# Three row outputs of set 8 in the buffers of the products E, and the rounded angle of the last two quarters in the tile u

## The chip, the core and the metric

The kernel runs on one core of one Trainium2 chip. The metric is the device time of one launch in microseconds (us). Five engines work side by side, each in the order of its own instructions: TensorE (PE in the profile, with its weight loads as PEld), VectorE (DVE), ScalarE (ACT), GpSimd (POOL) and SyncE (SP), which issues nearly all DMAs.

## What is computed

The reference is an adaLN block: a state space convolution (S4D) over 2048 tokens of 448 channels, and behind it a token-mixing MLP.

```python
x = A_u                                              # (1, 2048, 448)
sa, ca, ga, sb, cb, gb = modulation of c by w_mod
h = _layernorm(x) * (1 + ca) + sa
x = x + ga * _A_ref(h, ...)
h = _layernorm(x) * (1 + cb) + sb
x = x + gb * _B_ref(h, ...)                          # W2 gelu(W1 h), over the tokens
...
def _A_ref(u, log_A_real, A_imag, C_real, C_imag, log_dt, D_skip):
    dt = exp(log_dt); A = -exp(log_A_real) + 1j * A_imag; C = (C_real + 1j * C_imag) * dt
    P = exp((A * dt)[:, :, None] * pos)              # 448 channels x 256 modes x 2048 positions
    K = 2.0 * einsum("dn,dnl->dl", C, P).real
    y = irfft(rfft(u, 4096) * rfft(K, 4096))[:2048]
    return y + u * D_skip
```

## The kernel before

The kernel makes the convolution kernel K in 56 **steps** (two per group of 16 channels). A step s takes phases and magnitudes of 128 modes and makes two products: E (VectorE, lines 718 to 722) and G (GpSimd, lines 716 and 717). TensorE multiplies them into K two steps later (`st_kgen`, line 743). Eight steps are a **set** (sets 0, 8, 16, 24, ...). Ahead of each set stands a **window** (`window(s)`): ScalarE makes the eight magnitudes (`mag`, exponentials), and then changes its table for the sines of the steps. In a window no product is made, so E's buffers are idle there. E has three buffers of 128 x 2 x 16 x 64 floats, used in turn; step s takes the next one.

Other work is threaded between. In the windows of sets 8 and 16 and the steps behind them TensorE makes the **row outputs** of the spectrum of the input (`u_rows`, line 571): row outputs come in pairs, VectorE scales each of a pair out of PSUM into a tile `yt` (line 574), and a DMA writes the pair of 128 x 896 floats to DRAM (`yu_d`, line 576). There are 16 pairs, and `yt` has three buffers. Six of the pairs are made in the window of set 8. In the same window TensorE makes a first part of K's spectrum (`y`, line 781), which ScalarE copies (`yk`, line 787). PSUM has three banks for row outputs, modulation and `y` together (tag `ms`). From set 16 on the **column outputs** follow (`pu` at line 606, scaled into `uo` by VectorE at line 610).

The parameters come in four **quarters** q of 128 channels (the last has 64). `chain(q)` turns raw parameters into the tables that the phases need, a few VectorE instructions at a time. Its tiles have one buffer each per quarter. `split` takes a value apart into a rounded part and a rest (`hl`, lines 400 and 402, two buffers) and sends both to DRAM (`pars`, line 406); inside a window, and for q = 1, GpSimd does it, else VectorE. `phase` writes the tile `p64` and splits it; `angles` then rounds the angle `xa` into a tile and subtracts it (lines 438 and 440). For q = 1 `phase` stands ahead of the logarithms, for which u is needed afterwards; for q = 2 and 3 it stands at the end, when u is no longer needed but for the rounding inside `phase`.

The order on TensorE, ScalarE, VectorE and GpSimd is the order of the code (`manual_schedule`). SyncE's is so until step 8, and set by the framework's planner after that. Buffers of a pool are taken in turn; an instruction that writes a buffer waits for the last reader of what was in it.

Behind the steps come the products of the spectra (`pc_...`), a stretch with many transfers, then layernorm and the MLP, whose matmuls (lines 1377 to 1379 and 1540 to 1542) fill the last 270 us.

Of the kernel before, what the change touches and what calls it, by code (L numbers as in the profile page):

```python
# [11 lines left out]
F32 = mybir.dt.float32  # L12
# [3 lines left out]
ALU = mybir.AluOpType  # L16
# [5 lines left out]
L, D, N, F = 2048, 448, 256, 1792  # L22
P = 128
# [3 lines left out]
NI, NJ = 32, 64  # L27
GD = 16
# [5 lines left out]
MAGIC = 1.5 * 2.0**23  # L34
# [198 lines left out]
def tile_adaln_s4d_mixer(ctx, tc, i, out):  # L233
# [19 lines left out]
    with ExitStack() as es:  # L253
        V, S, G, T = nc.vector, nc.scalar, nc.gpsimd, nc.tensor
        tt, ts, stt = V.tensor_tensor, V.tensor_scalar, V.scalar_tensor_tensor
# [20 lines left out]
        xp = spec.enter_context(tc.tile_pool(name="xp", bufs=1))  # L276
# [110 lines left out]
        def chain(q):  # L387


            n = min(P, D - P * q)  # L390
            f = N * n // P
            cr, ci, a, aim = (raws[q][nm][:, 0:f] for nm in ("A_C_real", "A_C_imag", "A_log_A_real", "A_A_imag"))
            xa, ya, s, t, u, ph, p64 = (
                qp.tile([P, N], F32, tag=nm, name=nm)[:, 0:f] for nm in ("xa", "ya", "s", "t", "u", "ph", "p64")
            )

            def split(src, places):
                hl = qp.tile([P, 2, N], F32R, tag="hl", name="hl", bufs=2)[:, :, 0:f]
                eng = G if aside or q == 1 else V
                eng.tensor_copy(hl[:, 0], src)  # L400
                yield
                eng.tensor_tensor(hl[:, 1], src, hl[:, 0].bitcast(F32), ALU.subtract)
                for k, v in places:
                    for m in range(P // n):
                        to = pars[q][v, k, 0:n, :, m * f : (m + 1) * f]
                        nc.sync.dma_start(to, hl[n * m : n * m + n].bitcast(F32))
                yield


            def phase():  # L410
                ts(ph, aim, dt4[:, q : q + 1], None, ALU.mult)
                yield
                ts(u, ph, MAGIC, MAGIC, ALU.add, ALU.subtract)
                yield
                tt(ph, ph, u, ALU.subtract)
                yield
                yield from split(ph, [(0, 0)])

                ts(u, ph, MAGIC7, MAGIC7, ALU.add, ALU.subtract)
                yield  # L420
                tt(p64, ph, u, ALU.subtract)
                yield
                yield from split(p64, [(1, 0)])

            def angles():
                ts(xa, xa, 4 * i2p, -0.5, ALU.mult, ALU.add)
                yield
                ts(cr, cr, 0.0, 0.5, ALU.is_ge, ALU.subtract)
                yield
                tt(xa, xa, cr, ALU.mult)  # L430
                yield
                ts(ci, ci, 0.0, 0.5, ALU.is_ge, ALU.subtract)
                yield
                stt(xa, xa, 0.5, ci, ALU.add, ALU.mult)
                yield
                stt(xa, ph, 63.0, xa, ALU.mult, ALU.add)
                yield
                ts(p64, xa, MAGIC, MAGIC, ALU.add, ALU.subtract)
                yield
                tt(xa, xa, p64, ALU.subtract)  # L440
                yield
                yield from split(xa, [(2, 0)])

            for to, src in (xa, cr), (ya, ci):
                if q > 1:
                    S.activation(to, src, AF.Abs, scale=0.5)
                else:
                    ts(to, src, -0.5, None, ALU.mult)
                    yield
                    stt(to, src, 0.5, to, ALU.mult, ALU.max)  # L450
                    yield
            tt(s, xa, ya, ALU.add)
            yield
            tt(ya, ya, xa, ALU.subtract)
            yield
            ts(s, s, 2.0**-120, None, ALU.max)
            yield
            V.reciprocal(xa, s)
            yield
            tt(ya, ya, xa, ALU.mult)  # L460
            yield

            ts(t, s, 2.0**-40, 2.0**80, ALU.is_lt, ALU.mult)
            yield
            stt(s, t, 1.0, s, ALU.max, ALU.mult)
            yield
            if q == 1:
                while not late_steps:
                    yield "logs"
                yield from phase()  # L470
            tmp[q] = a, s, u, xa, ya
            while q in tmp:
                yield "logs"
            if q == 1:
                yield from angles()
            ya = u
            yield from split(a, [(0, 1), (1, 1)])
            stt(s, t, -80 * math.log(2.0) / 2.0**80, s, ALU.mult, ALU.add)
            yield
            stt(s, ya, 0.5, s, ALU.mult, ALU.add)  # L480
            yield
            ts(s, s, ldt2[:, q : q + 1], None, ALU.add)
            yield
            yield from split(s, [(2, 1)])
            yield "exponents"

            if q > 1:
                yield from phase()

            if q > 1:  # L490
                yield from angles()
# [59 lines left out]
            tt(rs, rs, nm, ALU.mult)  # L551
            ts(xt[:, :, D : D + 1], mv[:, :, 0:1], -1.0, None, ALU.mult)

        yts, wurs = {}, {}

        def u_table(R):
            wurs[R] = xp.tile([P, 2, P], F32, tag="wur", name="wur", bufs=3)
            scales = rs[:, 2 * R : 2 * R + 2, None].to_broadcast([P, 2, P])
            G.tensor_tensor(wurs[R], wu[:, None, :].to_broadcast([P, 2, P]), scales, ALU.mult)

        def u_rows(n):

            R, g = divmod(n, 4)
            gp, gl = divmod(g, 2)
            if gl == 0:
                yts[R, gp] = xp.tile([P, 2, D], F32, tag="yt", name="yt", bufs=3)
            if g == 0 and R < 6:
                u_table(R + 2)
            pm = pms.tile([P, D + 1], F32, tag="ms", name="pu")
            p = slice(64 * gl, 64 * gl + 64)  # L570
            T.matmul(pm, wurs[R][p, gp], xt[p, 2 * R + gp, 0 : D + 1], start=True, stop=True)

            def out():
                stt(yts[R, gp][:, gl], pm[:, 0:D], pm[:, D : D + 1], mod[1], ALU.add, ALU.mult)
                if gl:
                    nc.sync.dma_start(
                        yu_d[:, :, :, R, 2 * gp : 2 * gp + 2].rearrange("o k c g d -> (o k c) (g d)"),
                        yts.pop((R, gp)).rearrange("p g d -> p (g d)"),
                    )

            dve.append(out)
# [489 lines left out]
        def window(s):  # L1071
# [12 lines left out]
            for e in range(BATCH):  # L1084
# [33 lines left out]
                if s in (8, 16):  # L1118
                    some(u_rows, rows, ((0, 2, 2, 2, 2, 0, 2, 2) if s == 8 else (2, 2, 2, 2, 2, 0, 1, 1))[e])
                elif s == 24 and e in (0, 2, 4, 6, 7):  # L1120
                    some(u_cols, cols, 1)
# [21 lines left out]
        for s in range(NHALF):  # L1143
# [13 lines left out]
            if s % BATCH == 0:  # L1157
                (late_window if s > 32 else window)(s)
                if s == 0:
                    gp_ = right("gp", 3)  # L1160
# [56 lines left out]
            if 8 <= s < 16 and free:  # L1217
                some(u_rows, rows, 2 if s % 2 else 3)
# [47 lines left out]
        n = pieces[0]  # L1266
# [47 lines left out]
        for k in range(NP + 1):  # L1314

            n = NP + k
# [42 lines left out]
    with ExitStack() as es:  # L1359
# [169 lines left out]
        for t in range(16):  # L1529
# [4 lines left out]
            for kh in range(2):  # L1534
                n = 32 + 2 * t + kh
# [38 lines left out]
```

## Time and profile before

| | |
|---|---|
| median of 3 runs | 670.04 us (669.04 to 670.37) |
| profiled execution, time | 668.55 us |
| its span, first to last instruction | 666.7 us |
| TensorE busy | 615.8 us (92%) |
| VectorE busy | 442.9 us (66%) |
| ScalarE busy | 440.4 us (66%) |
| GpSimd busy | 269.7 us (40%), all of it in the first 55% of the span |
| mean granted TensorE clock | 0.978 |

Durations of single instructions are from the one profiled execution. A row of the timeline reads: start, length, engine, line, operation, output and inputs, size, count, and in brackets how long the engine was idle before and what ended that. In the chain of waits a row is start, length and what the time went to. A row of a stretch gives the busy time of each engine in it.

### The profile page before, as it was taken

To read this page: it belongs to the slowest core of one execution; us is meant where nothing else is said; L and a number is where in the kernel's file an instruction comes from. 1 tells how busy PE (TensorE), PEld (TensorE's weight loads), DVE (VectorE), ACT (ScalarE), POOL (GpSimd) and SP (SyncE) were. 2 spreads that over 40 slices of the span, in tenths; PEclk is the share of its full clock that TensorE was granted. 3 is DMA by queue.
4 is the path that set the end of the run, shared out by engine and by line. 5 is a ranking of instruction groups with operands and counts; after the bars stand their busy time and mean duration, and the time that the engine had idled before them with its cause. 6 is when DMAs were issued, how large, how long until landed. Compare 5 with 4: busy or idle time off the path is not lost.

```text
span 666.7 us, 19151 instructions
## 1 busy us (share of the span) xinstructions
PE 615.8 (92%) x7637; PEld 445.0 (67%) x7637; DVE 442.9 (66%) x850; ACT 440.4 (66%) x828; POOL 269.7 (40%) x349
## 2 busy tenths in 40 slices
PE   1868899999899999999989899999999999999997
PEld 0545455445346565656645577788999999999997
DVE  8989789689696686869655678787522553333331
ACT  6978698899689999999678678886222532222220
POOL 7885588488589878797463000000000000000000
PEclk9998899999899899999999899999999999999999
DMA  6696747598775458567787999946664265555530
GB/s 157 191 215 174 253 157 247 197 257 260 221 236 175 107 128 215 168 185 222 210 281 238 262 243 249 220 125 200 169 189 137 71 188 161 165 162 167 163 116 28
DMA packets 99601, 125.14 MB, mean 188 GB/s; under 512 B 13780, under 2 KB 81144, under 8 KB 99512
## 3 DMA queue, kind: packets, MB, share of 16 engines
q1 hardware_dynamic: 98568, 121.30, 63.9%
q0 software_dynamic: 944, 2.62, 1.6%
q8 instruction: 60, 0.98, 0.6%
q14 instruction: 29, 0.24, 0.1%
HBM read 88.53 MB, written 34.87 MB: 185 GB/s over the span
## 4 chain that ended last, share of the span: by engine, by line
PE 60%; DMA 13%; ACT 9%; POOL 6%; DVE 5%; issue 4%; SPq 2%; ACTq 0%; DVEq 0%; POOLq 0%
PE o L1541 7%; PE o L1540 7%; PE o L1542 7%; PE acc L1377 6%; PE acc L1378 6%; PE acc L1379 6%; PE xe L646 5%; PE kg L743 5%; DMA v_d<-vt 4%; DMA w<-in_B_w_dram 3%; PE xg L646 3%; DMA lph<-pars 2%; PE pu L606 2%; PE vv L874 2%; POOL G L716 2%
## 5 line engine op out<-in xcount | busy, mean ns | idle before, releaser
L218 ACT CAST whi<-w 128x896 fp32r<-128x896 f32 x64 | 59.7, 939 | 138.2 <-PE o L1541 81.3
L227 DVE TENSOR_TENSOR wlo<-w,whi 128x896 fp32r<-128x896 f32 x64 | 68.1, 1086 | 41.2 <-ACT whi L218 38.1
L716 POOL TENSOR_TENSOR G<-mag,gs 128x512 f32<-128x512 f32 x56 | 71.9, 1284 | 42.2 <-ACT gs L712 42.2
L1377 PE MATMUL acc<-h3h,whi 128*128 128x448 f32 x224 | 83.0, 370 | 2.4 <-ACT h3h L1444 0.9
L1378 PE MATMUL acc<-h3l,whi 128*128 128x448 f32 x224 | 81.6, 364 | 0.6 <-DVE h3l L1451 0.4
L1541 PE MATMUL o<-ul,whi 128*128 128x448 f32 x224 | 81.3, 363 | 0.0
L1540 PE MATMUL o<-uh,whi 128*128 128x448 f32 x224 | 81.2, 362 | 0.0
L1379 PE MATMUL acc<-h3h,wlo 128*128 128x448 f32 x224 | 80.7, 360 | 0.0
L1542 PE MATMUL o<-uh,wlo 128*128 128x448 f32 x224 | 80.6, 360 | 0.0
L743 PEld LDWEIGHTS kg<-E,G 128*32 128x32 f32 x3584 | 54.7, 112 | 30.2 <-issue 19.0
L717 POOL TENSOR_TENSOR G<-mag,gs 128x512 f32<-128x512 f32 x56 | 71.9, 1284 | 0.0
L646 PE MATMUL xg<-tab,lph 64*128 64x512 f32 x112 | 63.4, 566 | 8.2 <-DVE E L722 5.3
L743 PE MATMUL kg<-E,G 128*32 128x64 f32 x3584 | 63.9, 224 | 4.8 <-issue 3.4
L646 PE MATMUL xe<-tab,lph 64*128 64x512 f32 x112 | 63.5, 567 | 0.3 <-issue 0.2
L1545 DVE TENSOR_TENSOR y<-o,x 128x448 f32<-128x448 f32 x16 | 10.0, 627 | 78.9 <-PE o L1542 78.9
L696 POOL TENSOR_TENSOR m<-mag,w 128x512 f32<-128x512 f32 x53 | 55.8, 1053 | 4.1
L1377 PEld LDWEIGHTS acc<-h3h,whi 128*128 128x128 f32 x224 | 42.0, 188 | 16.1 <-ACT h L1449 2.8
L708 ACT ACTIVATE ab<-xe 128x512 f32<-128x512 f32 x56 | 33.8, 604 | 19.5 <-PE xg L646 10.2
L1378 PEld LDWEIGHTS acc<-h3l,whi 128*128 128x128 f32 x224 | 42.1, 188 | 3.6 <-DVE h3l L1451 1.0
L1540 PEld LDWEIGHTS o<-uh,whi 128*128 128x128 f32 x224 | 42.0, 188 | 3.4
L1542 PEld LDWEIGHTS o<-uh,wlo 128*128 128x128 f32 x224 | 41.9, 187 | 3.0
L1379 PEld LDWEIGHTS acc<-h3h,wlo 128*128 128x128 f32 x224 | 41.9, 187 | 2.9
(249 smaller groups left out, 1406.6 us busy)
## 6 DMA issues: line engine op xcount, KB each, us to landing
w<-in_B_w_dram SPq DMA_DIRECT2D x64, 224.0 KB
w<-in_B_w_dram SPq DMA_DIRECT2D x32, 448.0 KB
yu_d<-yt SPq DMA_DIRECT2D x16, 448.0 KB
yi<-yu_d SPq DMA_DIRECT2D x32, 224.0 KB
us_d<-uo SPq DMA_DIRECT2D x16, 448.0 KB
u<-us_d SPq DMA_DIRECT2D x64, 112.0 KB
v_d<-vt SPq DMA_DIRECT2D x32, 224.0 KB
vt<-v_d SPq DMA_DIRECT2D x14, 448.0 KB
```

Source lines behind the costliest of these rows:

```text
L218: self.nc.scalar.copy(hi, w)
L227: eng.tensor_tensor(lo, w, hi.bitcast(F32), ALU.subtract)
L646: T.matmul(out[k], lhs[r], rhs[r], start=start, stop=stop)
L716: G.tensor_tensor(Gt[:, 1], mg_, v32(sg), ALU.mult)
L717: G.tensor_tensor(Gt[:, 0], mg_, v32(cg_), ALU.mult)
L743: T.matmul(kg[32 * q : 32 * q + 32, m], Gt[:, c, d], E[:, c, d], start=h == 0 and c == 0 and m == 0, stop=h == 1 and c == 1, skip_group_ch ...
L1377: nc.tensor.matmul(acc[f], hi[:, fs], h3h[:, r], start=r == 0, stop=False)
L1378: nc.tensor.matmul(acc[f], hi[:, fs], h3l[:, r], start=False, stop=False)
L1379: nc.tensor.matmul(acc[f], lo[:, fs], h3h[:, r], start=False, stop=r == 15)
L1540: nc.tensor.matmul(o, hi[:, ks], uh[kh][:, k], start=kh == 0 and k == 0, stop=False)
L1541: nc.tensor.matmul(o, hi[:, ks], ul[kh][:, k], start=False, stop=False)
L1542: nc.tensor.matmul(o, lo[:, ks], uh[kh][:, k], start=False, stop=kh == 1 and k == 6)
```

## The change

Two edits. In `u_rows` the third, fourth and fifth pair of row outputs (counted from 0: pairs 2 to 4) are not written into `yt` but into two buffers that are taken from the pool of E: pairs 2 and 3 share one, pair 4 has the other. The buffers of `yt` are so taken by pairs 0, 1, 5, 6, ... in turn. In `angles` the rounded angle of the quarters 2 and 3 goes into u instead of p64.

```diff
@@ angles(), in chain(q)
-                ts(p64, xa, MAGIC, MAGIC, ALU.add, ALU.subtract)
+                whole = u if q > 1 else p64
+                ts(whole, xa, MAGIC, MAGIC, ALU.add, ALU.subtract)
                 yield
-                tt(xa, xa, p64, ALU.subtract)
+                tt(xa, xa, whole, ALU.subtract)
@@
-        yts, wurs = {}, {}
+        yts, wurs, lent = {}, {}, []
@@ u_rows(n)
             if gl == 0:
-                yts[R, gp] = xp.tile([P, 2, D], F32, tag="yt", name="yt", bufs=3)
+                pair = n // 2
+                if pair in (2, 4):
+                    E = gp_.tile([P, 2, GD, NJ], F32, tag="E", name="yE")
+                    rooms = E.rearrange("p a g j -> p (a g j)")[:, 0 : 4 * D].rearrange("p (h g d) -> p h g d", h=2, g=2)
+                    lent.extend(rooms[:, h] for h in range(2))
+                yts[R, gp] = lent[pair - 2] if 2 <= pair < 5 else xp.tile([P, 2, D], F32, tag="yt", name="yt", bufs=3)
```

No instruction changes its place on any engine, SyncE's queue included; what changes is what some of them wait for. In the rows below the names in brackets are the semaphores waited for: DMAHW0 to 7 stand for DMAs, the others for engines. Line numbers of the change are 1 to 6 higher.

VectorE in the window of set 8, before: the pairs of row outputs 1 to 4, with the start of the chain of q = 2 between the last two.

```order
L574 SCALAR_TENSOR_TENSOR yt<-pu,mod_105 128x448 [waits PE_49] x4
L574 SCALAR_TENSOR_TENSOR yt<-pu,mod_105 128x448 [waits DMAHW7_49,PE_49]
L574 SCALAR_TENSOR_TENSOR yt<-pu,mod_105 128x448 [waits PE_49]
L452 TENSOR_TENSOR s<-xa,ya 128x256 [waits DVE_49,Activation_49,Pool_49]
L454 TENSOR_TENSOR ya<-ya,xa 128x256 [waits DVE_49]
L456 TENSOR_SCALAR s<-s 128x256
L458 RECIPROCAL xa<-s 128x256 [waits DVE_49]
L460 TENSOR_TENSOR ya<-ya,xa 128x256 [waits DVE_49]
L463 TENSOR_SCALAR t<-s 128x256
L574 SCALAR_TENSOR_TENSOR yt<-pu,mod_105 128x448 [waits DMAHW0_49,PE_49]
L574 SCALAR_TENSOR_TENSOR yt<-pu,mod_105 128x448 [waits PE_49]
```

The same place now:

```order
L580 SCALAR_TENSOR_TENSOR yt<-pu,mod_105 128x448 [waits PE_49] x2
L580 SCALAR_TENSOR_TENSOR yE<-pu,mod_105 128x448 [waits PE_49] x4
L453 TENSOR_TENSOR s<-xa,ya 128x256 [waits DVE_49,Activation_49,Pool_49]
L455 TENSOR_TENSOR ya<-ya,xa 128x256 [waits DVE_49]
L457 TENSOR_SCALAR s<-s 128x256
L459 RECIPROCAL xa<-s 128x256 [waits DVE_49]
L461 TENSOR_TENSOR ya<-ya,xa 128x256 [waits DVE_49]
L464 TENSOR_SCALAR t<-s 128x256
L580 SCALAR_TENSOR_TENSOR yE<-pu,mod_105 128x448 [waits PE_49] x2
```

The waits for the DMAs of earlier pairs are gone from pairs 3 and 4 (counted from 0).

VectorE in the steps 9 and 10, now: the first products E that come into the borrowed buffers.

```order
L724 TENSOR_TENSOR E<-m_1112,xe 128x16x32 [waits DMAHW3_49,DMAHW2_49,Activation_49]
L725 SCALAR_TENSOR_TENSOR E<-mag,xe 128x16x32
L727 TENSOR_TENSOR E<-mag,xg 128x16x32 [waits Activation_49]
L728 TENSOR_TENSOR E<-m_1112,xg 128x16x32
L724 TENSOR_TENSOR E<-m_1353,xe 128x16x32 [waits DMAHW6_49,Activation_49,Pool_49]
```

Their waits for DMAHW3, DMAHW2 and DMAHW6 are new.

VectorE at the end of the window of set 24, before: the last instructions of `angles` for q = 3, and two pairs of column outputs.

```order
L436 SCALAR_TENSOR_TENSOR xa<-ph,xa 128x128 [waits DVE_49]
L438 TENSOR_SCALAR p_2172<-xa 128x128 [waits DVE_49,Pool_49]
L440 TENSOR_TENSOR xa<-xa,p_2172 128x128 [waits DVE_49]
L610 SCALAR_TENSOR_TENSOR uo<-mod_104,svt,pu 128x2x224 [waits DMAHW1_49,PE_49]
L610 SCALAR_TENSOR_TENSOR uo<-mod_104,svt,pu 128x2x224 [waits PE_49]
```

The same place now:

```order
L439 TENSOR_SCALAR u<-xa 128x128 [waits DVE_49]
L441 TENSOR_TENSOR xa<-xa,u 128x128 [waits DVE_49]
L616 SCALAR_TENSOR_TENSOR uo<-mod_104,svt,pu 128x2x224 [waits DMAHW1_49,PE_49]
L616 SCALAR_TENSOR_TENSOR uo<-mod_104,svt,pu 128x2x224 [waits PE_49]
L616 SCALAR_TENSOR_TENSOR uo<-mod_104,svt,pu 128x2x224 [waits DMAHW2_49,PE_49]
```

The wait for GpSimd (Pool) has gone from the rounding. The first products E of steps 24 and 25, and the first instruction of the next quarter's chain, carry a wait for GpSimd that the old row used to cover.

## The prediction

> **What bounds the kernel now.** I read the page first, then the chain of work that ended last, then the timeline around the two places that the change touches, and last the table of stretches.
>
> ```profile
> span 666.7 us, 19151 instructions
> PE 60%; DMA 13%; ACT 9%; POOL 6%; DVE 5%; issue 4%; SPq 2%; ACTq 0%; DVEq 0%; POOLq 0%
> ```
>
> The chain is mostly TensorE, but it changes hands. Around the first place, the window of set 8, it runs over these pieces:
>
> ```profile
> 70.94 5.08 DMA yu_d<-yt
> ...
> 76.12 0.70 DVE yt L574
> ...
> 82.92 1.28 ACT L711
> ```
>
> So the chain comes through a DMA that writes a row output to DRAM, because its buffer is wanted again. Two stretches behind the two places show what takes the time once the windows are over (columns: PE, PEld, DVE, ACT, POOL busy, each with its count, then the granted clock, DMA share, GB/s):
>
> ```profile
> 85.40:109.90 24.50, 23.79 (x458) 13.72 (x450) 22.46 (x38) 21.99 (x44) 24.03 (x27) 1.00 0.59 194
> 186.60:210.80 24.20, 23.27 (x570) 13.32 (x572) 23.35 (x40) 22.38 (x44) 23.77 (x25) 1.00 0.56 185
> ```
>
> GpSimd is busy 24.03 of 24.5 us in the first and 23.77 of 24.2 in the second. It has no gap worth the name there. So in both places a gain counts for exactly as much as it brings forward the product G that starts this unbroken run: the one at 85.38 (first step of set 8) and the one at 186.56 (second step of set 24).
>
> **Part 1: three row outputs in idle E buffers.** Rows of the window of set 8 (start, length, engine, line, idle time before and what ended it):
>
> ```profile
> 71.76 1.28 DVE L574 SCALAR_TENSOR_TENSOR yt<-pu,mod 128x448 f32<-128x448 f32 x2 [1.13 <-PE pu L571]
> 72.83 1.02 PE L571 MATMUL pu<-xt,wur 64*128 64x449 f32 x3
> 73.58 0.54 PE L571 MATMUL pu<-xt,wur 64*128 64x449 f32 x1
> 76.12 1.28 DVE L574 SCALAR_TENSOR_TENSOR yt<-pu,mod 128x448 f32<-128x448 f32 x2 [3.08 <-DMA yu_d<-yt]
> 76.86 1.16 PE L781 MATMUL y<-wc,ks 64*64 64x64 f32 x62 [2.26 <-DVE yt L574]
> 78.06 1.07 ACT L787 COPY yk<-y 128x512 f32<-128x512 f32 x2 [2.78 <-PE y L781]
> 79.51 0.62 ACT L675 ACTIVATE mag<-xg 128x512 f32<-128x512 f32 x1
> 81.82 0.60 ACT L708 ACTIVATE ab<-xe 128x512 f32<-128x512 f32 x1 [1.70 <-PE xe L646]
> 85.38 1.28 POOL L716 TENSOR_TENSOR G<-mag,gs 128x512 f32<-128x512 f32 x1 [8.12 <-ACT gs L712]
> 87.95 0.69 DVE L718 TENSOR_TENSOR E<-m,xe 128x512 f32<-128x512 f32 x1 [0.32 <-ACT xe L711]
> ```
>
> The pair at 76.12 is the fourth of the set. VectorE was free at 76.12 - 3.08 = 73.04; its first matmul result is there at 73.85 (72.83 + 1.02). Without the buffer wait it starts at about 73.9, as the pair before it started 0.03 us behind its own matmuls. That is 2.2 us earlier. Behind it in the same order: the matmuls y (they need a PSUM bank that this pair frees) go from 76.86 to about 74.65, the two copies yk on ScalarE from 78.06 to 75.85, the last exponentials from 79.51 to 77.3, ending at about 77.9. All of that is 2.2.
>
> The rest hangs on TensorE's clock:
>
> ```profile
> 75.00:78.40 3.40, 1.54 (x65) 1.37 (x66) 2.24 (x5) 0.62 (x2) 2.26 (x4) 0.96 0.63 250
> 78.40:81.80 3.40, 3.40 (x15) 2.48 (x14) 3.33 (x5) 1.73 (x4) 0.00 (x0) 0.54 1.00 296
> ```
>
> After a stretch with 1.54 us of work in 3.4, the next 3.4 us ran at a granted clock of 0.54, and in it lie the phase matmuls for which ScalarE waited 1.70 us at 81.82. Without the wait TensorE is idle for about 0.1 us instead of 2.26, and I take the full clock. At full clock the same matmuls stand in the profile too:
>
> ```profile
> 186.34 0.50 PE L646 MATMUL xe<-tab,lph 64*128 64x512 f32 x1
> 187.45 1.54 PE L606 MATMUL pu<-yi,s 64*64 64x448 f32 x8
> ```
>
> A whole phase takes 187.45 - 186.34 = 1.1 us. Then TensorE does y until 75.8, the exponents until 76.25, two row outputs (about 1.0, behind the copy yk that frees their bank at 76.4) until 77.4, the phase until 78.5. ScalarE is free at 77.9, so ab starts at 78.5 instead of 81.82: 3.3 us. The table load (82.92) and the sines follow it unchanged, so G moves from 85.38 to about 82.05. VectorE is no hindrance: its products E go with the sines. **Term: -3.3 us**, with bounds -2.2 (clock drops anyway) and -3.9 (81.82 to 77.9, ScalarE never waiting for a phase).
>
> [...]
>
> What it costs. The number of instructions and their shapes are the same, so their time is zero on every engine. The two borrowed buffers belong to steps 9 and 10, whose first products now wait for the DMAs of pairs three to five. The product of step 9 stood at 87.95 and would come at 84.65. The DMA of the fourth pair would be issued behind that of the third, at about 75.9:
>
> ```profile
> 75.47 2.28 SPq L576 DMA_DIRECT2D yu_d<-yt  x2
> 82.07 0.34 SPq L576 DMA_DIRECT2D yu_d<-yt  x1
> ```
>
> With the 5.08 us of the chain's row it lands at about 81, 3.6 us ahead of its reader. The fifth pair goes out near 80 instead of 82.07 and lands at 85, its reader comes near 88.7. Behind a waiting product would stand the other E products on VectorE and the kernel matmuls on TensorE; I cost it at nothing, since the cover is 3.6 us. On the DMA queue nothing changes place; its issues come 1.5 to 3 us earlier, into a stretch with a DMA share of 0.63.
>
> **Part 2: the rounded angle in u.** Only the last quarter's matters: of three such instructions one waited. Rows of the window of set 24:
>
> ```profile
> 173.77 0.29 DVE L436 SCALAR_TENSOR_TENSOR xa<-ph,xa 128x128 f32<-128x128 f32 x1
> 175.88 0.29 POOL L400 CAST hl<-p 128x128 fp32r<-128x128 f32 x1 [4.20 <-DMA pars<-hl]
> 176.74 0.23 DVE L438 TENSOR_SCALAR p<-xa 128x128 f32<-128x128 f32 x1 [2.68 <-POOL hl L402]
> 177.21 1.27 DVE L610 SCALAR_TENSOR_TENSOR uo<-mod,svt,pu 128x448 f32<-128x448 f32 x2
> 177.94 1.01 PE L606 MATMUL pu<-yi,s 64*64 64x448 f32 x3 [2.23 <-DVE uo L610]
> 178.94 0.29 POOL L400 CAST hl<-xa 128x128 fp32r<-128x128 f32 x1 [2.23 <-DMA pars<-hl]
> 180.48 1.98 PE L781 MATMUL y<-wc,ks 64*64 64x64 f32 x62 [0.78 <-DVE uo L610]
> 182.51 1.05 POOL L696 TENSOR_TENSOR m<-mag,w 128x512 f32<-128x512 f32 x1
> 184.39 0.60 ACT L708 ACTIVATE ab<-xe 128x512 f32<-128x512 f32 x1 [5.05 <-PE xg L646]
> 186.56 1.29 POOL L716 TENSOR_TENSOR G<-mag,gs 128x512 f32<-128x512 f32 x1 [3.00 <-ACT gs L712]
> ...
> 177.40:184.00 6.60, 5.29 (x78) 3.17 (x78) 3.85 (x7) 1.94 (x4) 4.46 (x6) 0.50 0.85 248
> ```
>
> VectorE waits 2.68 us to overwrite p64, which GpSimd still has to split, and GpSimd waits for a DMA. With u the wait goes: 176.74 becomes 174.06, uo starts near 174.55, the matmuls pu near 175.2, y near 176.75, at full clock (the 6.6 us at 0.50 followed the 2.23 us gap) the phase ends near 179, and ab would stand at 179.1 instead of 184.39, 5.3 us earlier. But GpSimd doesn't get all of that. Its cast at 178.94 waits for a DMA that the change doesn't touch, and its products and the m at 182.51 follow that cast without a gap. It is free at 183.56, and G there starts at 183.56 instead of 186.56. **Term: -3.0 us**, which is just the idle time in that row. Even at half clock ab would come some 1.5 us later, still early enough for 183.56. The bounds are 0 (the gap is filled by something that the trace doesn't show) and -5.3 (GpSimd's wait shrinks too). Two E products of that set and the first instruction of the next quarter get a wait on GpSimd; what they wait for was made before the cast at 175.88, so it costs nothing.
>
> **Sum:** -3.3 - 3.0 = -6.3 us. The profiled execution took 668.55 us (span 666.7 plus 1.85), which is 1.49 below the median 670.04; I take the sum off the median: 663.7. What is won early should stay won, as I see no transfer on the chain behind these places that was issued ahead of them.
>
> **Rivals.**
> *The clock stays low* after the first place: 2.2 instead of 3.3, sum -5.2, 664.8. For it speaks that the slow stretch is a whole 3.4 us long and may not hang on this gap alone; against it that 1.54 us of work went ahead of it.
> *One place pays alone.* If the first fails 667.0, if the second fails 666.7. For it: SyncE's in-order issue could move a DMA on which GpSimd waits. Against: its order is the same.
> *The gain is given back* where the transfers bound the kernel:
>
> ```profile
> 382.56 10.19 DMA w<-in_B_w_dram
> ...
> 342.00:394.00 52.00, 46.21 (x383) 28.53 (x375) 32.75 (x81) 36.43 (x74) 10.26 (x19) 0.97 0.91 259
> ```
>
> A DMA share of 0.91 over 52 us speaks for it. Against it: these weight loads are issued by code behind the spectrum's products and move with them. It would give 670.0.
> *Slower:* the product of step 9 waits for the borrowed buffer. From a landing at 84.65 on, every further microsecond holds VectorE. VectorE has 24.5 - 22.46 = 2.0 us of slack in that set. To end 1.3 us above the median it must land 6.3 + 2.0 + 1.3 = 9.6 us late, at 94.3, 18 us after its issue. If it took 20 us (95.9) the result would be 670.0 - 6.3 + 11.2 - 2.0 = 672.9. The 5.08 us row speaks against it.
>
> **How the numbers follow.** The forecast has 0.64, the low clock 0.12, one place alone 0.11, given back 0.09, slower 0.04. About 0.2% (1.3 us) is what a measurement can tell from no change. Faster are the first three: 0.87; the given-back case makes 0.09 the same, and 0.04 is slower. The range starts at 670.0 - 3.3 - 5.3 = 661.4 (the second term's far bound) and ends at 667.8, where only the 2.2 of the first place is left; that leaves out the last two cases and a little more.
>
> **What would show it.** Right: no wait of the row outputs on yu_d in set 8, y near 74.7, a granted clock of 1.00 over 78 to 82, G near 82; in set 24 no wait of the rounding on GpSimd, G of the second step right behind m with no idle time, and everything behind 190 earlier by 6 us. Wrong: a wait of an E product on yu_d in set 8; a longer idle time of GpSimd at the cast of xa; or a stretch behind 212 that has grown by what was won.

## The result, and the profile after

The changed kernel took 665.09 us (median of 9 runs, 662.59 to 668.58), the kernel before 670.04 (9 runs, 666.82 to 670.49). The ratio is 0.9941, 95% interval 0.9914 to 0.9967; a ratio is the comparison's own estimate and need not be the quotient of the two medians. Two later comparisons of the same two kernels (below) gave 0.9968 (0.9933 to 1.0003) and 0.9998 (0.9967 to 1.0030). The mean of the three is 0.9969, or 2.1 us: a gain, but a third of the one forecast. That the first comparison lies in the range of the forecast (661.4 to 667.8) is in part luck: taken off 670.04, the ratios of the other two give 667.9 and 669.9, which lie outside it. The profiled execution took 665.80 us; its span is 664.0 us against 666.7.

The window of set 8 looks as forecast. Rows of its timeline, after (start, length, engine, line, operation, idle time before and what ended it):

```profile
71.17 1.28 DVE L580 SCALAR_TENSOR_TENSOR yE<-pu,mod 128x448 f32<-128x448 f32 x2 [0.64 <-PE pu L577]
73.77 1.29 DVE L580 SCALAR_TENSOR_TENSOR yE<-pu,mod 128x448 f32<-128x448 f32 x2 [1.31 <-PE pu L577]
74.52 1.15 PE L787 MATMUL y<-wc,ks 64*64 64x64 f32 x62 [0.29 <-DVE yE L580]
75.71 1.07 ACT L793 COPY yk<-y 128x512 f32<-128x512 f32 x2 [0.62 <-PE y L787]
78.09 0.60 ACT L714 ACTIVATE ab<-xe 128x512 f32<-128x512 f32 x1 [0.31 <-PE xe L652]
81.65 1.28 POOL L722 TENSOR_TENSOR G<-mag,gs 128x512 f32<-128x512 f32 x1 [6.50 <-ACT gs L718]
84.22 0.69 DVE L724 TENSOR_TENSOR E<-m,xe 128x512 f32<-128x512 f32 x1 [0.32 <-ACT xe L717]
```

The pair that waited 3.08 us for a DMA now waits for its matmul, y starts at 74.52 instead of 76.86, and G at 81.65 instead of 85.38. The product E of step 9 (84.22) comes into a borrowed buffer and waits for ScalarE, not for a DMA. The clock stayed full (columns as in the table of stretches before; third from the end is the granted clock):

```profile
75.00:78.40 3.40, 3.40 (x62) 2.14 (x53) 3.30 (x7) 2.47 (x6) 0.15 (x1) 1.00 0.80 256
78.40:81.80 3.40, 2.71 (x17) 1.49 (x18) 3.40 (x8) 3.37 (x6) 0.15 (x1) 1.00 0.85 300
```

Then something new. In the sixth step of the set a later pair of row outputs waits for a buffer of `yt` (timeline of after, SyncE's issues and VectorE's wait):

```profile
95.02 0.41 SPq L337 DMA_DIRECT2D xt<-in_w_mod_dram  x1
95.52 2.76 SPq L582 DMA_DIRECT2D yu_d<-yt  x2
...
103.64 1.28 DVE L580 SCALAR_TENSOR_TENSOR yt<-pu,mod 128x448 f32<-128x448 f32 x2 [2.15 <-DMA yu_d<-yt]
```

The chain of waits (start, length, what the time went to) passes here:

```profile
95.52 8.03 DMA yu_d<-yt
...
103.64 0.70 DVE yt L580
```

The row output issued at 95.52 stands on the chain for 8.03 us, where the one in the window before had 5.08. It was issued 0.5 us behind a load of modulation weights (`xt<-in_w_mod`, 784 KB).

In set 24, timeline of after:

```profile
170.67 0.29 DVE L436 SCALAR_TENSOR_TENSOR xa<-ph,xa 128x128 f32<-128x128 f32 x1
170.99 0.23 DVE L439 TENSOR_SCALAR u<-xa 128x128 f32<-128x128 f32 x1
173.95 1.15 PE L787 MATMUL y<-wc,ks 64*64 64x64 f32 x62 [0.77 <-DVE uo L616]
176.31 0.60 ACT L714 ACTIVATE ab<-xe 128x512 f32<-128x512 f32 x1
177.12 0.29 POOL L400 CAST hl<-xa 128x128 fp32r<-128x128 f32 x1 [3.18 <-DMA pars<-hl]
177.90 1.27 POOL L722 TENSOR_TENSOR G<-mag,gs 128x512 f32<-128x512 f32 x1
180.69 1.05 POOL L702 TENSOR_TENSOR m<-mag,w 128x512 f32<-128x512 f32 x1
181.70 1.29 POOL L722 TENSOR_TENSOR G<-mag,gs 128x512 f32<-128x512 f32 x1
```

The rounding into u waits for nothing, and G of the second step (181.70) comes right behind m. GpSimd's wait at the cast of `xa` is longer than before, 3.18 us instead of 2.23.

Every run behind the prediction left a profile too. The table gives, for each, the waits of row outputs on their DMAs near 75 us and near 104 us, and the starts of the first products G of steps 8, 15, 16, 24 and 25, of GpSimd's last step (55) and of the last copy `h3h` (layernorm's output, ScalarE); all in us. "Rows" means pairs 2 to 4 in E's buffers, "u" the rounding in u, "hl" and "load" are edits explained below. In the three kernels with "load" the later wait comes near 112 us instead: 2.44 us in e5, 0.48 and 0.72 in e7, 2.57 in e8.

| kernel | edits | wait 75 | wait 104 | G8 | G15 | G16 | G24 | G25 | G55 | h3h | span |
|---|---|---|---|---|---|---|---|---|---|---|---|
| before | none | 3.08 | 0 | 85.38 | 112.60 | 135.38 | 179.72 | 186.56 | 321.66 | 451.83 | 666.7 |
| after | rows, u | 0 | 2.15 | 81.65 | 109.79 | 132.67 | 177.90 | 181.70 | 317.31 | 449.09 | 664.0 |
| e1_again | rows, u | 0 | 2.26 | 82.85 | 114.05 | 136.92 | 181.60 | 185.39 | 321.32 | 452.65 | 667.6 |
| e9_after | rows, u | 0 | 2.06 | 82.35 | 113.02 | 136.26 | 180.80 | 184.61 | 320.34 | 449.24 | 664.2 |
| e2_part1 | rows | 0 | 2.37 | 82.00 | 112.74 | 135.95 | 180.47 | 186.44 | 321.60 | 451.26 | 666.2 |
| e3_part2 | u | 1.43 | 1.98 | 82.62 | 113.22 | 136.16 | 180.59 | 184.38 | 320.11 | 451.50 | 666.4 |
| e10_part2 | u | 0 | 2.47 | 84.90 | 114.36 | 137.37 | 182.63 | 186.44 | 322.38 | 452.97 | 667.9 |
| e4_warm8 | matmuls | 2.42 | 0.9 | 83.39 | 110.56 | 133.17 | 179.39 | 186.35 | 321.18 | 451.56 | 666.5 |
| e5_wm_later | rows, u, load | 0 | 0 | 81.83 | 109.08 | 134.62 | 179.67 | 183.46 | 319.10 | 450.70 | 665.6 |
| e7_both | rows, u, hl, load | 0 | 0 | 82.76 | 110.00 | 136.21 | 179.69 | 183.49 | 319.36 | 449.06 | 664.0 |
| e8_part2_wm | u, load | 0 | 0 | 82.85 | 110.13 | 134.57 | 178.95 | 182.76 | 318.61 | 449.78 | 664.7 |
| e6_hl_lent | rows, u, hl | 0 | 1.20 | 81.26 | 109.42 | 132.62 | 176.44 | 180.25 | 316.15 | 444.97 | 659.9 |
| e11_hl_lent | rows, u, hl | 0 | 0.72 | 80.92 | 110.11 | 132.99 | 175.63 | 179.43 | 315.48 | 445.96 | 660.9 |
| e12_hl_only | u, hl | 1.62 | 1.36 | 84.71 | 112.11 | 134.99 | 178.78 | 182.59 | 318.21 | 450.73 | 665.6 |

### The profile page after: what moved, and what is told of

Its sections match the earlier page's. It is cut to its first block, busy times and chain, and to the rows that moved or that the text cites. A ratio compares the mean times of both kernels' runs of the same rounds, so it can differ in the third digit from the quotient of the medians.

```text
span 664.0 us, 19150 instructions
## 1 busy us (share of the span) xinstructions
PE 611.2 (92%) x7637; PEld 442.4 (67%) x7637; DVE 444.5 (67%) x850; ACT 440.9 (66%) x828; POOL 269.8 (41%) x349
## 4 chain that ended last, share of the span: by engine, by line
PE 70%; ACT 8%; DMA 7%; DVE 6%; issue 4%; POOL 3%; SPq 1%; DVEq 0%; ACTq 0%; POOLq 0%
PE xe L652 8%; PE o L1548 7%; PE o L1547 7%; PE o L1546 7%; PE acc L1383 6%; PE kg L749 6%; PE acc L1384 6%; PE acc L1385 6%; PE xg L652 4%; PE vv L880 2%; DMA w<-in_B_w_dram 2%; PE pu L612 2%; PE pu L577 2%; PE kx L857 2%; PE y L787 1%
## 5 line engine op out<-in xcount | busy, mean ns | idle before, releaser
L1547 PEld LDWEIGHTS o<-ul,whi 128*128 128x128 f32 x224 | 42.0, 188 | 3.4
```

The source lines that it names most:

```text
L1547: nc.tensor.matmul(o, hi[:, ks], ul[kh][:, k], start=False, stop=False)
```

## The experiments

The theory was that the row outputs' transfers are one backlog: taking away the wait near 75 lets another appear later, which the kernel before did not meet because its set 8 ran later, so that the first edit brings little and the second nearly all. The rival was the prediction's sum, in which both terms reach the end.

**Again, and each edit alone.** The three ran on one chip, against 668.74 us for the kernel before (35 runs).

e1_again is the changed kernel.

> The changed kernel once more, as the yardstick of this chip and as a second profile. If the traced gain is a property of the kernel, the first product G of set 8 comes near 82 and that of the second step of set 24 near 182 again, and the median lies 4 to 6 us under the kernel before. If what was lost behind set 24 (4.9 us ahead at 182, 2.7 us ahead at the end) is a property of the kernel, the lead shrinks again by 2 us behind 190; if it was chance in one execution, it shrinks by another amount.

665.94 us, ratio 0.9968 (0.9933 to 1.0003). By the medians it is 2.8 us under the kernel before, where 4 to 6 were expected, and G of the second step of set 24 came at 185.39, not near 182. So much of the lead in the profile of after (4.86 us at this place) belonged to that execution and not to the kernel.

e2_part1 has only the row outputs in E's buffers:

```diff
-                whole = u if q > 1 else p64
+                whole = p64
```

> Only the row outputs in the E buffers; the rounded angle stays in p64 for all quarters. Theory of two separate terms: G of set 8 near 82 as in the changed kernel, the wait of the rounding on GpSimd in set 24 back (2 to 3 us), and some 2.3 us (3.2 less the 0.9 that set 8 gives back at its end) under the kernel before, near 667.7. Rival, one term is all: as fast as the changed kernel (665), or no faster than before (670).

667.80 us, ratio 0.9984 (0.9956 to 1.0012).

e3_part2 has only the rounding in u:

```diff
-                yts[R, gp] = lent[pair - 2] if 2 <= pair < 5 else xp.tile([P, 2, D], ..., bufs=3)
+                yts[R, gp] = xp.tile([P, 2, D], ..., bufs=3)
```

> Only the rounded angle in u for the last two quarters; the row outputs stay in yt. Theory of two separate terms: the 3.1 us wait of the fourth pair on its DMA stays in set 8, no wait of the rounding in set 24, GpSimd without idle time ahead of the G of the second step there, 2.2 to 3.0 us under the kernel before, near 667.4. Rival: GpSimd's wait for the DMA at the cast of the angle grows by what is won, and the time stays at 670.

665.74 us, ratio 0.9968 (0.9941 to 0.9995). The rounding alone does as much as the whole change; the row outputs alone differ from no change by less than the interval (0.9 us of median, where an edit that pays by itself was to bring 2.3). The rows of the second wait, of e2 and then of e3 (timeline):

```profile
104.23 1.29 DVE L580 SCALAR_TENSOR_TENSOR yt<-pu,mod 128x448 f32<-128x448 f32 x2 [2.37 <-DMA yu_d<-yt]
```

```profile
74.74 1.28 DVE L575 SCALAR_TENSOR_TENSOR yt<-pu,mod 128x448 f32<-128x448 f32 x2 [1.43 <-DMA yu_d<-yt]
104.47 1.28 DVE L575 SCALAR_TENSOR_TENSOR yt<-pu,mod 128x448 f32<-128x448 f32 x2 [1.98 <-DMA yu_d<-yt]
```

So the second wait does not need the first edit. And the first wait, 3.08 us in the one profile that the prediction had, is 1.43 here with the same row-output code.

**The clock by itself.** e4_warm8 is the kernel before with 16 matmuls that compute nothing needed, ahead of y, where TensorE stood idle:

```diff
+                    if s == 8:
+                        warm(16)
                     st_s1(act)
```

> The kernel before with 16 idle matmuls on TensorE (about 2 us, into a bank that nobody reads) at the place in the window of set 8 where it waits for the row output. The wait of 3.1 us itself stays. Theory (the 2.26 us gap drops the clock, which costs 1.1 us there): granted clock 1.00 over the 3.4 us behind the gap, the phase's matmuls at full speed, G of set 8 near 84.3 instead of 85.38, and a time 1 us lower, which the interval may not show. Rival (a gap of that length is too short to matter): the clock is 0.5 for a stretch behind it as before, G near 85.4 or later.

667.96 us, ratio 1.0000 (0.9967 to 1.0032). The wait on the DMA is kept, and the clock is full behind it (timeline and table of stretches of e4; the same stretches of before had 0.96 and 0.54):

```profile
75.51 1.28 DVE L574 SCALAR_TENSOR_TENSOR yt<-pu,mod 128x448 f32<-128x448 f32 x2 [2.42 <-DMA yu_d<-yt]
```

```profile
75.00:78.40 3.40, 3.40 (x82) 2.75 (x80) 2.82 (x6) 1.27 (x3) 1.70 (x3) 1.00 0.79 312
78.40:81.80 3.40, 2.75 (x15) 1.12 (x11) 3.37 (x7) 3.07 (x6) 0.00 (x0) 1.00 0.72 210
```

That speaks for TensorE's idle time (2.26 us in before) as the cause of that slow stretch, by one execution of each kernel; the last section has the longer idle times of all fourteen. G8 came 2.0 us earlier than before, but not by the clock alone: the wait was 0.66 shorter too, and in this kernel the planner issued two of the row outputs' DMAs at other places between the loads of the parameters (81.65 and 85.99 instead of 82.07 and 84.69). At the end nothing is left of it.

**The load out of the way.** Is the load of 784 KB what makes the second wait? In e5_wm_later a small write by GpSimd to the load's tile holds the load back until GpSimd gets there; the planner then issues two row outputs ahead of it that stood behind it:

```diff
-            13: lambda: wm_load(5, xt[0:PP, 4:8, 0:D]),
+            13: lambda: [G.memset(xt[0:1, 4, 0:1], 0.0), wm_load(5, xt[0:PP, 4:8, 0:D])],
```

> The changed kernel with the 784 KB load of the modulation's weights (k = 5) held back in set 8: a one-element memset on GpSimd ahead of step 13's products lets it start some 7 us later, behind two DMAs of row outputs instead of ahead of them. Theory (the second wait of a row output, 2.1 to 2.4 us near 104, comes from transfers queued behind this load and gives back most of what the first edit won): no or a much smaller wait there, the set from its first to its last G 27 to 28 us instead of 28 to 31, and 1 to 3 us under the changed kernel. Rival (the wait is the price of three buffers at this pace, whatever goes ahead): a wait of 2 us stays somewhere in the set and the time is that of the changed kernel.

667.57 us, ratio 0.9980 (0.9949 to 1.0010), on a chip where the kernel before took 668.07 (35 runs). The load went out at 102.70 instead of 95.02. No row output waits near 104 any more, and one does 7 us later (timeline of e5):

```profile
102.70 0.35 SPq L337 DMA_DIRECT2D xt<-in_w_mod_dram  x1
103.14 0.92 SPq L582 DMA_DIRECT2D yu_d<-yt  x2
...
105.19 1.28 DVE L580 SCALAR_TENSOR_TENSOR yt<-pu,mod 128x448 f32<-128x448 f32 x2
111.29 1.88 DVE L580 SCALAR_TENSOR_TENSOR yt<-pu,mod 128x448 f32<-128x448 f32 x3 [2.44 <-DMA yu_d<-yt]
```

From G8 to G15 it took 27.25 us (28.14 in after, 30.67 to 31.20 in e1 and e9), but from G15 to G16 25.54 (22.88 in after). The wait went with the load. The time did not follow: 1 to 3 us under the changed kernel were expected, and the ratio is not under the changed kernel's 0.9941 to 0.9998. The same edit beside two other combinations says the same of the wait.

e8_part2_wm has the rounding in u and the later load, with row outputs in `yt`:

> The second edit and the later load of the modulation's weights, without the first edit (the row outputs stay in yt). Theory (both waits of row outputs are real, and the first edit takes away the one, the load's place the other): the first wait stays (1.4 to 3.1 us near 75), the second is small, and it is slower than e5 by 1.4 to 3 us. Rival (the two waits are one backlog of transfers, which whichever comes first pays): the same time as e5.

666.33 us, ratio 0.9958 (0.9936 to 0.9981); G8 to G15 27.28, G15 to G16 24.44. The first wait, expected to stay, was absent in this execution, with the row outputs in `yt`; the late one was 2.57. It was to be 1.4 to 3 us slower than e5 and was not: its median is 1.2 lower. e7_both is e5 with the next experiment's edit:

> The last two together: if both places are on the path, their gains add, 3.5 to 5 us under the changed kernel (near 661 where that is 665); if one hides the other, no better than the better of the two.

667.27 us, ratio 0.9976 (0.9949 to 1.0002); 27.24 and 26.21. The expected sum of two gains (3.5 to 5 us) is not there. In these runs the load's place went with where the row outputs wait, near 104 or near 112 us (0.48 to 2.57 us there), not with whether they do.

**The cast's buffer.** The second place still had GpSimd's wait at the cast of `xa` (3.18 us in after). It waits for the DMA of an earlier `hl`, which has two buffers. e6_hl_lent is the changed kernel, and for the last quarter's `xa` takes a buffer of E, idle in the window, in place of one of `hl`:

```diff
-            def split(src, places):
-                hl = qp.tile([P, 2, N], F32R, tag="hl", name="hl", bufs=2)[:, :, 0:f]
+            def split(src, places, lend=False):
+                if lend:
+                    E = gp_.tile([P, 2, GD, NJ], F32, tag="E", name="hE")
+                    hl = E... [:, 0 : 2 * N] ... .bitcast(F32R)
+                else:
+                    hl = qp.tile([P, 2, N], F32R, tag="hl", name="hl", bufs=2)[:, :, 0:f]
...
-                yield from split(xa, [(2, 0)])
+                yield from split(xa, [(2, 0)], q == 3)
```

> The changed kernel with the split of the last quarter's angle written into an idle E buffer too, so that GpSimd's cast needs not wait for the DMA of an earlier split. Theory (after the second edit GpSimd's wait at this cast, 3.2 us, bounds the start of set 24): no wait at that cast, the first G of set 24 directly behind ScalarE's sines, some 2.5 us earlier than in the changed kernel, and 2.5 us less in all. Rival (the set's start hangs on another engine): the cast's wait goes, the G of the second step stays where it was, and the time stays.

665.06 us, ratio 0.9954 (0.9927 to 0.9980). No wait is left at the cast, and from G16 to G25 it took 47.63 us, 1.4 less than after (49.03), where 2.5 were expected.

**Two by two on one chip.** Whether the first edit brings anything, and whether the cast's buffer does, was then measured together: rounding in u in all four, row outputs in E or in `yt`, cast in E or in `hl`. Before took 668.33 us (35 runs).

> The changed kernel, as the partner of the three beside it. Together they make a table of two by two: the row outputs in E's buffers or not, the cast's buffer lent or not, with the rounding in u in all four. Theory A (one backlog of row outputs, paid early or late): this kernel and the one with the rounding alone differ by no more than 0.2%. Rival (the row outputs bring their 3 us): this kernel is 0.4% faster than the rounding alone.

> The rounding in u alone, row outputs in yt as before. Theory A: within 0.2% of the whole change. Rival: 0.4% slower than it, only 0.2 to 0.3% faster than before.

> The whole change, and the cast of the last quarter's angle in an idle buffer of E. If the cast's DMA wait is what is left of the second place, 1.4 to 2.5 us (0.2 to 0.4%) faster than the change itself; if the gain is taken back behind set 24, equal to it.

> The rounding in u and the cast in an idle buffer of E, row outputs in yt as before. Theory A: equal within 0.2% to the kernel that has the row outputs in E as well, and as the best with one edit fewer. Rival: 0.4% slower than that one.

| rounding in u, and | cast in hl | cast in E |
|---|---|---|
| row outputs in E | e9: 668.71 us, 0.9998 (0.9967 to 1.0030) | e11: 664.54 us, 0.9936 (0.9907 to 0.9965) |
| row outputs in yt | e10: 667.67 us, 0.9971 (0.9945 to 0.9998) | e12: 664.61 us, 0.9936 (0.9908 to 0.9964) |

Down the columns: the row outputs in E are worth +1.0 and -0.1 us of median, that is nothing that shows. With the three other pairs that ran on one chip (e2 against before -0.9, e1 against e3 +0.2, e5 against e8 +1.2) the mean of five is +0.3 us, and none comes near the -3.3 of the forecast. Across the rows: the cast's buffer is worth 4.2 and 3.1 us. GpSimd's rows of e12 in the window of set 24 show where (timeline):

```profile
175.86 0.46 POOL L406 TENSOR_TENSOR hl<-p,hl 128x128 fp32r<-128x128 f32 x1
176.27 0.29 POOL L404 CAST hE<-xa 128x128 fp32r<-128x128 f32 x1
176.63 0.45 POOL L406 TENSOR_TENSOR hE<-xa,hE 128x128 fp32r<-128x128 f32 x1
178.78 1.28 POOL L721 TENSOR_TENSOR G<-mag,gs 128x512 f32<-128x512 f32 x1 [1.69 <-ACT gs L717]
```

The cast follows the split ahead of it at once. In its place GpSimd waits 1.69 us for ScalarE, so a part of the 3.18 remained as the next wait: from G16 to G25 e6, e11 and e12 took 46.44 to 47.63 us, mean 47.22, which is 1.4 less than the five that at this place have the rounding but not this edit (after, e1, e3, e9, e10: 48.63). The medians show more than that, and where the rest comes from is not shown. In the profiles the three stand 3.7 us ahead of the five at G55, but 2.3 of these already at G16, where the edit has not yet begun to work: chance of the executions is mixed into such leads. e12, with one edit fewer than e11, is as fast: of the kernels run it is the one to keep. With the later load (e7 against e5) the cast's buffer moved the median by only 0.3 us; why it was less there stays open.

## Why the prediction was right and wrong

**Term 2 (3.0 us) was right.** Its steps were that VectorE's wait goes, that ScalarE comes early enough, and that GpSimd's cast bounds the gain, so that exactly the idle 3.00 us ahead of G of the second step are won. From G24 to G25 it took 6.84 us before, 5.97 in e2 and 6.96 in e4; it is 3.79 to 3.81 in all eleven profiles with the rounding in u. From G16 to G25 the three without it took 51.18, 50.49 and 53.18 us, the five just named 48.22 to 49.07, mean 48.63: 3.0 us less than the mean of the three, which scatter by 2.7. In after alone, the gain from G16 to G25 is 2.15, as the cast's DMA wait grew by 0.95; the prediction's "a longer idle time of GpSimd at the cast" was seen there and in e9 (3.08) and e10 (2.92), but not in e1 (2.29) or e3 (1.97). In the times it is 2.1 and 1.9 us (e3 and e10 against before, by their ratios), and 1.1 (e1 against e2).

Behind G25 some of it is gone again: from there to G55 the three profiles without the rounding took 134.8 to 135.2 us, the eleven with it 135.6 to 136.1, 0.8 more on the mean. The larger part of that lies in the window of set 32, where ScalarE waits for the phase. Its rows in before and in after (timeline):

```profile
218.75 0.60 ACT L708 ACTIVATE ab<-xe 128x512 f32<-128x512 f32 x1 [0.32 <-PE xe L646]
214.38 0.60 ACT L714 ACTIVATE ab<-xe 128x512 f32<-128x512 f32 x1 [0.82 <-PE xe L652]
```

In nine of the fourteen profiles this wait is 0.82 to 0.85 us, in before and e2 0.32 and 0.38, in e4, e6 and e12 0.12. In after, one of the nine, a stretch at a granted clock of 0.50 begins at 212.70, 9.3 us behind G31; in before one begins at 218.09, 9.8 us behind it. That the place of this stretch makes the difference, or that the edit itself moves it, is not shown.

**Term 1 (3.3 us) was right at its place and gone at the end.** y at 74.52 (forecast 74.7), the clock at 1.00, G at 81.65 (forecast 82.05), no wait of E products: each step of it held up to there. Two steps behind it failed. One is "a gain counts for exactly as much as it brings forward the product G that starts this unbroken run": the run did not stay unbroken. From G8 to G15 GpSimd was idle for 0.47 us in before, and for 1.36 in after and 1.35 to 4.47 in the five others with row outputs in E and the load where it was (3.82 and 2.71 in e3 and e10, with row outputs in `yt`). The other is "What is won early should stay won, as I see no transfer on the chain behind these places that was issued ahead of them". The search was for transfers already on the chain. The one that mattered stood on no chain of before: the three `yt` buffers turn over through the same DMAs for 50 us more, and what the first wait does not hold back, the second does.

In the five executions with row outputs in `yt` and the load where it was (before, e3, e4, e10, e12) the two waits add up to 3.08, 3.41, 3.3, 2.47 and 2.98 us, however they divide; in the six with row outputs in E, to 2.15, 2.26, 2.06, 2.37, 1.20 and 0.72. So the room lent to three pairs shortens the two waits by 1.3 us on the mean (3.05 against 1.79), not by 3.08. And where half clock followed it a wait went with more than its length: e1, e2 and e9, with a granted clock of 0.50 for 6.8 us behind it, took 3.4 to 4.0 us longer than before from G8 to G15, for waits of 2.06 to 2.37. The six have G8 at 81.84 on the mean, 2.6 us ahead of the four with row outputs in `yt` and no added matmuls (84.40); with e5, e7 and e8, whose later load comes behind G8, it is 2.1. At G15 1.6 are left (111.52 against 113.07), at G16 1.4 (134.57 against 135.98), where single executions of either group differ by more than 2 us. Of that the times show nothing: e2 against before -1.1 us by its ratio, with an interval that holds zero, e9 against e10 and e11 against e12 +1.0 and -0.1 of median.

A second fault lies in the size. The sum took 3.08 us from one execution. With the same code the first wait was 2.42 in e4, 1.62 in e12, 1.43 in e3, and not there in e10 and e8. So this wait, from 0 to 3.08 us, isn't a constant of the kernel.

**The rivals.** One place alone was given 0.11, with 667.0 us if the first place failed; that is nearest to what the three comparisons showed (670.04 less 2.1 is 667.9), in the form that a part of its gain is paid back later in its own set and no time shows the rest. The prediction's reason for it, a SyncE issue that moves another DMA, is not what was seen. Given back where the weights are loaded is not needed for this: from G55 to the last `h3h` the kernels took 128.8 to 132.5 us, before 130.17, and both ends belong to kernels with the rounding in u (e6 and e12). After lost 1.6 us there and e9 won 1.3 with the same code, so this stretch scatters, whatever the edit. From the last `h3h` to the end of the span it is 214.9 to 215.0 us in all. The low clock (0.50) did come in some executions, at another place (last section). The slower rival, E waiting for a DMA, was not seen in any of the fourteen profiles.

**What stays open.** The first comparison gave 0.9941, the third 0.9998. The profile of after is one of the fortunate executions: its second wait was followed by a full clock (1.00), and it took 28.14 us from G8 to G15, where e1, e2 and e9, with 0.50 behind that wait, took 30.67 to 31.20. Why the clock stayed full there is not shown, and whether that explains the larger first ratio can't be said from one profile of nine runs. Nor is it settled whether the first edit is worth the 1.4 us of the profiles at G16 or nothing.

## What to carry to other kernels

When a wait on a buffer goes, follow the same buffers to their last use: the transfers that freed them late are still there, and a wait that the trace does not show may have been hidden by the one that it does show (here 2.15 us near 104, where 3.08 near 75 had gone). A wait ended by the engine's own order (a tile that another engine has yet to read) is won up to the next bound, which is the next row to look at (here GpSimd's cast, and behind it ScalarE); a wait on a DMA can differ from execution to execution (here 0 to 3.08 us with the same row-output code), and its size should be taken from several profiles.

## What the runs showed of the hardware

Behind most of the longer idle times of TensorE its granted clock was half, but not behind each. Between 70 and 118 us the timelines of TensorE of the fourteen profiles have eleven idle times of 1.57 to 3.26 us. By the tables of stretches a granted clock of 0.50 came behind nine of them, for 3.4 us (before, e8, e10, e11) or 6.8 (e1, e2, e3, e9, and in e5 at least 6.0, where the table ends); behind two (1.82 in after, 1.63 in e6) none came.

Stretches of before, of e9 (idle for 1.74 us) and of after (idle for 1.82):

```profile
74.73:78.14 3.41, 1.28 (x64) 1.21 (x65) 1.99 (x5) 0.63 (x3) 2.53 (x4) 1.00 0.60 237
78.14:81.55 3.41, 3.41 (x14) 2.42 (x13) 3.34 (x7) 1.99 (x4) 0.00 (x0) 0.50 0.96 291
```

```profile
102.21:105.62 3.41, 1.67 (x9) 0.67 (x6) 1.34 (x3) 2.81 (x6) 3.41 (x5) 1.00 0.94 374
105.62:109.03 3.41, 3.41 (x68) 1.98 (x66) 3.41 (x7) 0.38 (x1) 3.33 (x4) 0.50 0.70 215
109.03:112.45 3.42, 3.42 (x13) 1.84 (x12) 1.58 (x3) 1.59 (x4) 0.52 (x2) 0.50 1.00 288
```

```profile
100.06:103.47 3.41, 2.51 (x50) 1.17 (x38) 1.43 (x3) 2.78 (x6) 3.33 (x5) 1.00 0.98 380
103.47:106.89 3.42, 2.50 (x70) 1.53 (x72) 3.25 (x6) 1.61 (x3) 3.34 (x5) 1.00 0.47 168
```

In before TensorE was busy for 0.38 of the 3.41 us ahead of the low stretch, in e9 for 0.49. In after the idle time (102.57 to 104.39) lies in both rows; together they are busy for 0.73, and the clock is 1.00 in both. What decides whether the clock drops, and for how long, is not shown. An idle time of that length was not needed everywhere: in before a clock of 0.50 came for 3.41 us at 115.69 too, behind idle times of 0.21 to 0.60 us, and at 218.09, behind 3.41 us in which TensorE reads busy throughout; in after it came at 212.70, behind 3.41 us that read so too.

The kernels whose set 8 lost the clock for 6.8 us with the load where it was (e1, e2, e3, e9) took 30.60 to 31.20 us from G8 to G15, after 28.14, which by estimate prices the longer drop at 2.5 to 3.1 us.

The other number is a transfer's time to land. A row output of 448 KB stood 5.08 us on the chain of waits in before, in the window of set 8, and 8.03 us in after, issued 0.50 us behind a load of 784 KB.
